# Linear attention on one core: the waits for the last stores, in GpSimd's stream or in SyncE's

## The chip, the cores and the metric

The kernel runs on one core of one Trainium2 chip. The metric is the device time of one execution in microseconds (us); several executions are made and their median is given.

## The reference

For 32 heads of 2048 rows and 128 columns in bf16, the kernel computes linear attention with the feature map elu(x) + 1:

```python
phi_q = jnp.where(q > 0, q + 1, jnp.exp(q)) + 1e-6
phi_k = jnp.where(k > 0, k + 1, jnp.exp(k)) + 1e-6
kv  = jnp.einsum("bhsd,bhse->bhde", phi_k, v)
z   = jnp.einsum("bhsd->bhd", phi_k)
num = jnp.einsum("bhqd,bhde->bhqe", phi_q, kv)
den = jnp.einsum("bhqd,bhd->bhq", phi_q, z)[..., None] + 1e-6
return num / den
```

Each head reads 512 KB each of q, k and v and writes 512 KB of output.

## The kernel before

Each head is one pass of the same operations. Its 2048 rows are laid out as 128 partitions with 16 rows each. SyncE (SP in the profile) issues every DMA of the kernel: 96 loads (`ldq`, `ldk`, `ldv`, line 324) and 34 stores (`st`, line 418). ScalarE (ACT) takes the exponentials of k and of the transposed q, a part of the positive parts, and the copy of the small matrix kv out of PSUM. VectorE (DVE) finishes the feature maps and, at the end of a head, takes the reciprocal of the denominators (line 403) and multiplies (line 410) into the output buffer. GpSimd (POOL) does two things for each head: `v1`, a copy of v beside a column of ones (line 350), and `rkp`, the positive part of half of k (line 346). TensorE (PE) makes kv (line 357), transposes q (line 368) and makes the numerators with their denominators (lines 389 to 396).

The order of every engine's work is written out by hand in `ORDER`, one string for each engine. POOL's string ends with `v131.0 rkp31.0`, the preparation of the last head's k and v. SP's string ends with the stores `st20.0` to `st30.0` and then the three partial stores of the last head, `st31.0 st31.1 st31.2`. `Program.resolve` turns the dependences into waits on semaphores: every engine has one semaphore of its own, and every DMA buffer has one. `Program.emit` writes each engine's stream, with `wait_ge` ahead of the instruction that needs it. There are five independent streams, and a wait holds only what stands behind it in its own stream.

There are twelve output buffers (NO = 12), and so twelve store semaphores, `o0` to `o11`. Head h uses buffer h mod 12; each store adds 16 to its buffer's semaphore when it has landed. After all streams are written, lines 433 to 435 add twelve waits, one for each store semaphore at its final count, the last one for `o7`, the buffer of head 31. They are the last instructions of the kernel; nothing of the kernel stands behind them. The compiler puts two waits into one instruction, so that six EVENT_SEMAPHORE instructions come out of the twelve. In the trace the last two of them wait for `o11` with `o1`, and for `o7` with `o0`.

Of the kernel before, what the change touches and what calls it, by code (L numbers as in the profile page):

```python
# [240 lines left out]
def bass_standalone__linear_attn_elu__prompt_kernel(nc: bass.Bass, q: bass.AP, k: bass.AP, v: bass.AP, out: bass.AP):  # L241
# [11 lines left out]
    with ExitStack() as es:  # L253
# [24 lines left out]
        pr = Program(sem)  # L278
# [153 lines left out]
            pr.emit(e, engine)  # L432
        last = f"o{(NH - 1) % NO}"
        for name in [f"o{s}" for s in range(NO) if f"o{s}" in pr.count and f"o{s}" != last] + [last]:
            nc.sync.wait_ge(pr.get(name), pr.count[name])


# [26 lines left out]
```

## Time and profile before

| what | value |
|---|---|
| median of 5 runs | 170.31 us (169.68 to 170.90) |
| the profiled execution's own time | 169.93 us |
| its span, from the first to the last instruction | 168.5 us |
| busy share of the span | PE 94%, DVE 92%, ACT 91%, POOL 51% |
| granted TensorE clock | 1.00 |
| DMA | 401 GB/s as a mean over the span |

The span is what the profile shows of the kernel's own instructions. The time of the execution is about 1.4 us longer, for what lies around the span. Waits and DMA issues are not counted as busy. The engine names carry a "q" (SPq, POOLq) where an instruction is one of the engine's sequencer alone, such as a wait or a DMA issue.

### The profile page before, as it was taken

The numbers are of one execution on the slowest core, as the hardware profiler recorded it, in microseconds if no ns is written. First come the engines' busy times: TensorE is split into PE (matmuls) and PEld (weight loads), VectorE is DVE, ScalarE is ACT, GpSimd is POOL, SyncE is SP. The second block draws the span as 40 slices with busy tenths as digits, with TensorE's granted clock in tenths as the row PEclk, the third lists the DMA queues.
The fourth block names the chain that finished last, engine by engine and source line by source line (L and its number), as shares of the span: only waits on it lengthen the run. The fifth ranks groups of instructions, "written<-read, shape, count | busy, mean of one in ns | idle before, by whom it ended". The sixth has DMA issues, their size and how long they took to land.

```text
span 168.5 us, 6310 instructions
## 1 busy us (share of the span) xinstructions
PE 159.2 (94%) x2775; PEld 153.4 (91%) x2775; DVE 154.3 (92%) x267; ACT 153.9 (91%) x133; POOL 86.8 (51%) x71
## 2 busy tenths in 40 slices
PE   6989889999999999999999999999999999999960
PEld 2579879999999999999999999999999999999950
DVE  0178999999999999999999999999999999999893
ACT  3799989999999999999999999999999999997810
POOL 1446826556655556556555566555655565445000
PEclk9999999999999999999999999999999999999999
DMA  5999999999999999999999999999999999999986
GB/s 196 381 417 413 409 405 409 409 407 409 415 414 411 408 413 418 415 414 422 406 416 413 414 419 414 411 418 414 421 411 421 412 414 420 414 416 415 396 332 239
DMA packets 18748, 67.53 MB, mean 401 GB/s; under 512 B 2080, under 2 KB 2464, under 8 KB 18720
## 3 DMA queue, kind: packets, MB, share of 16 engines
q1 hardware_dynamic: 18720, 67.12, 98.7%
q8 instruction: 22, 0.36, 0.8%
q14 instruction: 6, 0.05, 0.1%
HBM read 50.33 MB, written 16.78 MB: 398 GB/s over the span
## 4 chain that ended last, share of the span: by engine, by line
PE 83%; DVE 10%; ACT 4%; issue 1%; POOL 0%; POOLq 0%
PE la L357 31%; PE la L394 18%; PE la L396 16%; PE la L368 15%; DVE la L410 5%; ACT la L336 2%; PE la L315 2%; DVE la L342 1%; DVE la L339 1%; ACT la L372 1%; PE la L389 1%; DVE la L374 1%; DVE la L403 1%; DVE la L381 1%; ACT la L378 1%
## 5 line engine op out<-in xcount | busy, mean ns | idle before, releaser
L410 DVE TENSOR_TENSOR la<-la 128x1536 bf16<-128x1536 f32 (+2 forms) x65 | 77.5, 1194 | 0.2
L396 PE MATMUL la<-la 128*128 128x129 bf16 x512 | 68.1, 220 | 0.0
L394 PE MATMUL la<-la 128*128 128x129 bf16 x512 | 68.0, 219 | 0.0
L372 ACT ACTIVATE la<-la 128x2048 bf16<-128x2048 bf16 (+2 forms) x35 | 60.3, 1732 | 5.4 <-PE la L368 3.3
L357 PE MATMUL la<-la 128*128 128x129 bf16 x1024 | 64.0, 219 | 0.7 <-DVE la L339 0.7
L350 POOL COPY la<-la 128x1024 int32<-128x1024 int32 (+1 forms) x33 | 41.7, 1264 | 38.4 <-DVE la L403 29.3
L336 ACT ACTIVATE la<-la 128x2048 bf16<-128x2048 bf16 (+1 forms) x33 | 61.3, 1862 | 0.0
L357 PEld LDWEIGHTS la<-la 128*128 128x128 bf16 x1024 | 60.0, 97 | 1.3 <-DVE la L339 0.8
L346 POOL TENSOR_SCALAR la<-la 128x1024 bf16<-128x1024 bf16 x32 | 44.5, 1392 | 29.0 <-DVE la L410 24.9
L396 PEld LDWEIGHTS la<-la 128*128 128x128 bf16 x512 | 49.5, 97 | 0.0
L394 PEld LDWEIGHTS la<-la 128*128 128x128 bf16 x512 | 47.1, 97 | 0.0
L389 PE MATMUL la<-la 128*128 128x3 bf16 (+1 forms) x192 | 32.3, 168 | 2.4 <-DVE la L410 1.6
L368 PE MATMUL la<-la 128*128 128x128 bf16 x512 | 33.7, 219 | 0.4 <-DVE la L381 0.4
L378 ACT ACTIVATE la<-la 128x1024 bf16<-128x1024 bf16 (+1 forms) x32 | 33.6, 1049 | 0.0
L368 PEld LDWEIGHTS la<-la 128*128 128x128 bf16 x512 | 29.3, 97 | 1.3 <-DVE la L381 0.5
L339 DVE TENSOR_SCALAR la<-la 128x2048 bf16<-128x2048 bf16 (+1 forms) x33 | 23.2, 704 | 3.2 <-ACT la L336 3.2
L389 PEld LDWEIGHTS la<-la 128*128 128x128 bf16 x192 | 18.7, 97 | 3.6 <-DVE la L410 2.3
L374 DVE TENSOR_SCALAR la<-la 128x2048 bf16<-128x2048 bf16 (+2 forms) x35 | 21.2, 608 | 0.3 <-ACT la L372 0.3
L342 DVE TENSOR_SCALAR la<-la 128x1024 bf16<-128x1024 bf16 x32 | 17.1, 534 | 4.5 <-DMA la<-in_k_dram 4.5
L381 DVE TENSOR_SCALAR la<-la 128x1024 bf16<-128x1024 bf16 x31 | 20.8, 670 | 0.0
L403 DVE RECIPROCAL la<-la 128x12 f32<-128x12 f32 (+2 forms) x65 | 12.7, 196 | 2.2 <-PE la L396 0.9
L362 ACT ACTIVATE la<-la 128x129 bf16<-128x129 f32 x32 | 9.0, 282 | 0.4 <-PE la L357 0.4
(14 smaller groups left out, 11.7 us busy)
## 6 DMA issues: line engine op xcount, KB each, us to landing
la<-in_q_dram SPq DMA_DIRECT2D x32, 512.0 KB, 15.5
la<-in_k_dram SPq DMA_DIRECT2D x32, 512.0 KB, 15.3
la<-in_v_dram SPq DMA_DIRECT2D x32, 512.0 KB, 15.3
out_dram<-la SPq DMA_DIRECT2D x31, 512.0 KB, 15.2
out_dram<-la SPq DMA_DIRECT2D x2, 192.0 KB, 2.5
out_dram<-la SPq DMA_DIRECT2D x1, 128.0 KB, 2.6
```

What stands on the lines that cost most here:

```text
L336: add("ACT", f"ek{h}.{i}", lambda e, a=a, b=b: e.activation(em_sb[:, h % NE, a:b], k_sb[:, h % NI, a:b], ACT.Exp), over("ldk", h, ld_parts ...
L339: add("DVE", f"em{h}.{i}", lambda e, a=a, b=b: e.tensor_scalar(em_sb[:, h % NE, a:b], em_sb[:, h % NE, a:b], 1.0, EPS, op0=ALU.min, op1=AL ...
L346: add("POOL", f"rkp{h}.{i}", lambda e, a=a, b=b: e.tensor_scalar(rk_sb[:, h % NR, a:b], k_sb[:, h % NI, a:b], BIG, 0.0, op0=ALU.min, op1=A ...
L350: add("POOL", f"v1{h}.{i}", lambda e, a=a, b=b: e.tensor_copy(v1_sb[:, h % NV, a:b, 0:D].bitcast(i32), v_sb[:, h % NI, a:b].bitcast(i32)), ...
L357: ins = e.matmul(kv_ps, lhsT=src[:, j], rhs=v1_sb[:, h % NV, j, 0:NC], start=(j + part == 0), stop=(j == NT - 1 and part == 1))
L368: ins = e.transpose(xT[:, j], q_sb[:, h % NI, j], ident[:])
L372: add("ACT", f"eq{h}.{i}", lambda e, a=a, b=b: e.activation(emq_sb[:, h % NQ, a:b], xT[:, a:b], ACT.Exp), over("T", h, t_parts, a, b) + fr ...
L378: add("ACT", f"rqa{h}", lambda e: e.activation(rq_sb[:, h % NQ, 0:n], xT[:, 0:n], ACT.Relu), over("T", h, t_parts, 0, n) + freed(NQ, h, (" ...
L389: e.matmul(_ap(o_ps[:, :], o + D, [[NC, m]]), lhsT=ones[:], rhs=epsr[:, 0:m], start=True, stop=False, skip_group_check=True)
L394: e.matmul(to, lhsT=emq_sb[:, h % NQ, t], rhs=kvs_sb[:, h % NK], start=False, stop=False, skip_group_check=True)
L396: ins = e.matmul(to, lhsT=rq_sb[:, h % NQ, t], rhs=kvs_sb[:, h % NK], start=False, stop=True, skip_group_check=True)
L410: return e.tensor_tensor(out=_ap(o_sb[:, :, :, :], first(o_sb[:, h % NO, t0, 0:1]) - first(o_sb[:, :, :, :]), [[m * D, nb], [D, m], [1, D] ...
```

## The change

One word is changed. The same twelve waits, for the same semaphores and the same counts in the same order, are written into GpSimd's stream behind its last operation `rkp31.0`, and no longer into SyncE's behind its last store `st31.2`. SyncE's stream then ends with the issue of that store. Nothing else differs.

```diff
         last = f"o{(NH - 1) % NO}"
         for name in [f"o{s}" for s in range(NO) if f"o{s}" in pr.count and f"o{s}" != last] + [last]:
-            nc.sync.wait_ge(pr.get(name), pr.count[name])
+            nc.gpsimd.wait_ge(pr.get(name), pr.count[name])
```

## The prediction

> **What bounds the kernel now.** I read the page first, then only its last 20 us, because the moved waits are the last instructions of a stream: how many, when they run, what releases them, and what the engine that takes them is doing then. On the page, POOL's row of 40 slices of 4.2 us ends in three zeros, while DMA is busy to the end:
>
> ```profile
> span 168.5 us, 6310 instructions
> ...
> POOL 1446826556655556556555566555655565445000
> ...
> DMA  5999999999999999999999999999999999999986
> ```
>
> The table of windows gives the same with numbers. Each engine's entry is its busy time and, in brackets, its instructions: POOL has none after 156 us, and after 166 us no engine has any; only the stores are under way.
>
> ```profile
> 156.00:164.00 8.00, 6.52 (x120) 6.20 (x117) 7.19 (x13) 3.94 (x5) 0.00 (x0) 1.00 0.90 361
> 164.00:166.00 2.00, 0.16 (x3) 0.00 (x0) 1.83 (x5) 0.00 (x0) 0.00 (x0) 1.00 0.86 329
> 166.00:168.50 2.50, 0.00 (x0) 0.00 (x0) 0.00 (x0) 0.00 (x0) 0.00 (x0) 1.00 0.52 188
> ```
>
> The timeline (start, duration) has POOL's last operation, from 153.51 to 154.93 us, the last two multiplications on DVE, and three of the last stores' issues on SP:
>
> ```profile
> 153.51 1.41 POOL L346 TENSOR_SCALAR la<-la 128x1024 bf16<-128x1024 bf16 x1 [0.45 <-DVE la L410]
> ...
> 164.17 2.02 SPq L418 DMA_DIRECT2D out_dram<-la  x3
> 164.30 1.53 DVE L410 TENSOR_TENSOR la<-la 128x768 bf16<-128x768 f32 x2
> ```
>
> Then the answer for line 435, SP's waits, and the page's row for the last store:
>
> ```profile
> L435 SPq EVENT_SEMAPHORE  x6: 27/28/28, 167.2 to 168.5; - x6
> ```
> ```profile
> SPq L435 <- DMA out_dram<-la: 2.0, 2, 1.0
> ```
> ```profile
> out_dram<-la SPq DMA_DIRECT2D x1, 128.0 KB, 2.6
> ```
>
> Six instructions of 28 ns, the first at 167.2 us and the last at 168.5 us; they stood 2.0 us in all for two landings (1.0 us each) and not at all for the others. So **the end is set by** DVE's last multiplication (ends 165.83), the issue of `st31.2` (165.86 to 166.19), its landing (168.465 by the trace's semaphore records, 2.6 us after the issue began) and the wait that it releases (starts 168.481, ends 168.509). The waits themselves are 6 x 28 = 168 ns, of which only the last 28 ns lie behind the landing.
>
> **What surrounds the span.** The profiled execution took 169.93 us, 1.42 us over its span. The trace's semaphore records run on past the span: the last is at 169.938, equal to that time within 0.01 us. I read from this that the clock stops at the end of the closing barriers, and that what the streams do there counts. The barrier's semaphore has these updates (us from the span's start; the names are my reading of the order):
>
> ```
> first closing barrier:  164.340 PE, 164.374 ACT, 164.412 POOL, 165.987 DVE, 168.624 SP,
>                         then back: 168.667, 168.706, 168.740, 168.787
> second closing barrier: 169.581, .615, .653, .696, .720, then back: .819, .857, .891, .938
> ```
>
> In the first, four updates came early, one by one, as PE, then DVE, ran out of work (DVE's 156 ns after its last multiplication). The fifth came 115 ns after SP's last wait, and four more followed at 34 to 47 ns. In between the user semaphores are reset.
>
> **What the Trainium skill says.** "Runtime: NRT & Kernel Launch", section "The ~15µs preamble/postamble breakdown", describes a closing barrier, a reset of 51 semaphores by each engine and another barrier, and prices the barrier as a serpentine over the five engines at 44 ns a hop. The trace agrees on the form and the hop (34 to 47 ns); the reset took 0.61 us here (168.751 to 169.356) where the page says about 1.5. "Perfetto Trace Analysis", section "Summary: the profiler window per engine type", says that a sequencer's instruction shows only its execution, with the wait hidden ahead of it. That agrees with the 28 ns instructions and their 1.0 us of waiting, and it is why a long wait on POOL won't show as busy time. "DMA: Bandwidth & Descriptors", section "Why a DMA increments its semaphore by 16 and not by 1", says that each DMA engine adds one to the semaphore after its own data has landed; which engine of the core watches the semaphore is no part of the transfer. The trace has POOL and DVE wait on DMA semaphores of transfers that SP issued, so that works.
>
> **The change part by part.**
>
> *Removed from SP:* six instructions x 28 ns. Five lie ahead of the last landing (167.16 to 167.46) and are hidden by it; 28 ns and the 16 ns wake-up lie on the end path. No DMA is issued or moved, and nothing of SP's stands behind them. SP reaches the closing barrier after 166.19 and waits there.
>
> *Added to POOL:* six instructions behind `rkp31.0`, reached at about 154.95 us. The trace has POOL execute one with a single semaphore in 17 ns and one with two in 43 ns (line 217 has 17/17/43). It will pass pairs whose stores have landed and stand at the others; buffers `o0` to `o6` get their last stores between 159.35 and 167.15, and by 168.4 only `o7` is open. Five x 43 = 215 ns are hidden by the 1.0 us between the last two landings. Behind the waits POOL has no work, issues no DMA, and nobody of the kernel waits for it. No transfer, buffer release or other engine moves, so everything up to 168.465 stays.
>
> *The end path:* landing to POOL's wait 24 ns (ten such cases on POOL; SP 16), the wait 43 (SP 28): +23 ns.
>
> *The barrier:* POOL now comes third in a row of five but last in time. Before, its step was long done and SP's arrival at once began the way back. Now POOL's arrival is passed to DVE (+43 ns, as in the second barrier), to SP (+24), and then comes the turn (99 ns in the second barrier, where DVE too has just stepped) in place of the 43 ns of the first. Extra: 43 + 24 + 99 - 43 = **+123 ns**.
>
> *POOL's step out of its stream:* SP needs 115 ns from its last wait to its update. POOL's is not shown: it followed ACT's update by 38 ns after 9.5 us of idleness. Bounds: below, 60 ns, about half of SP's 115, the quickest seen here; above, the whole hidden 9.5 us. The nearest rows are SP's 115, DVE's 156 and POOL's own DRAIN at the opening:
>
> ```profile
> L449 POOLq DRAIN  x1: 187/187/187, 0.3 to 0.3; - x1
> ```
>
> I take 187, so +72 ns (-55 at the low bound).
>
> Sum: 23 + 123 + 72 = **+0.22 us**, against the profiled execution 169.93 + 0.22 = 170.15 us, with the span itself +0.02. This execution lay 0.38 us under the median, so the forecast stands on the median: 170.31 + 0.22 = 170.53, rounded to **170.5 us**, +0.13%. The measurement can tell about 0.5% (0.85 us) from no change; this lies inside.
>
> **The rivals.**
>
> *No part of the closing counts (chance 0.3):* the time ends with the last landing, or POOL's exit is as quick as SP's. Then +0 to +0.1 us, 170.3 to 170.4. For it: the landing is the same in both. Against: the agreement of 169.93 with the last record.
>
> *Slower, POOL's exit is long (chance 0.08):* POOL may have closing work of its own (its cores, or instructions to be fetched: the page has a queue of six instruction packets, one of them at 165.3 us). Before, up to 9.5 us of it was hidden between 154.93 and 164.41. If it begins only after the last wait, it is exposed. It decides when the exit exceeds 115 + 850 - 146 = about 0.82 us. A fetch priced like the kernel's shortest DMA round trip, 2.2 us, gives 170.31 + 0.15 + 2.2 - 0.1 = 172.6. Against: POOL steps through the second barrier in 38 ns, and it stands 12 us in its waits, time enough to fetch ahead.
>
> *Faster (chance 0.03, by spread):* SP's exit leaves the path. At most the 159 ns of its wake-up, last wait and exit could be saved, and POOL's own steps take their place; with a 60 ns exit the sum is still +0.09. Nothing here reaches 0.85 us; only the spread of the runs (169.68 to 170.90) could.
>
> *The edit does nothing:* if the compiler moved the waits to another stream, 170.3. The six instructions under line 435 tell.
>
> **How the numbers follow.** The likeliest, a shift of +0.1 to +0.3 us, has 0.57 and the case of no shift 0.30: 0.87 within 0.5%. The long exit has 0.08; the spread of the runs alone could carry the result over the bound, 0.02 upward and 0.03 downward. The five runs reach 0.63 below and 0.59 above their median, so I take 0.7 on both sides: **169.8 to 171.2 us**; the long exit is left out. Chances: faster 0.03, same 0.87, slower 0.10.
>
> **What would show it.** Right: six EVENT_SEMAPHORE of line 435 on POOLq, the first long before 167 us, the last about 25 ns after the last landing and 43 ns long; none on SPq; span 168.5 plus run-to-run spread; 0.2 us more between span and time (1.42 to about 1.6). Wrong: a gap between span and time of 2.2 us or more (the long exit), an unchanged 1.42 (no shift), or other engines' work before 165.8 us running differently.

## The result, and the profile after

| | before | after |
|---|---|---|
| median | 170.32 us (80 runs) | 170.92 us (43 runs) |
| ratio to before | | 1.0035, 95% interval 1.0024 to 1.0045 |
| the profiled execution's own time | 169.93 us | 170.99 us |
| its span | 168.51 us | 169.15 us |

The change costs 0.35%, which is 0.60 us (0.41 to 0.77). That is inside the 0.5% that the prediction called no change, and inside its range. It is nearly three times the +0.22 us forecast, and the interval of the ratio lies clear of the +0.13% that this would have been.

The span, three windows by engine (busy time, instructions in brackets), and SP's waits for the last 20 us, all of the kernel after:

```profile
span 169.2 us, 6310 instructions
```
```profile
156.00:164.00 8.00, 6.52 (x120) 6.21 (x117) 7.27 (x13) 3.94 (x5) 0.00 (x0) 1.00 0.84 339
164.00:166.00 2.00, 0.42 (x8) 0.24 (x5) 2.00 (x5) 0.00 (x0) 0.00 (x0) 1.00 0.92 358
166.00:169.20 3.20, 0.00 (x0) 0.00 (x0) 0.09 (x1) 0.00 (x0) 0.00 (x0) 0.88 0.46 168
```
```profile
SPq L418 <- DVE la L403: 12.2, 4, 4.7
SPq L418 <- DVE la L410: 3.5, 3, 2.6
```

The last stretch has the same shape: but for the end of DVE's last multiplication every engine has run out, and only stores are under way. That end comes 0.26 us later than in the kernel before (166.089 us against 165.831). It doesn't follow the moved waits: over the five kernels whose last wait stands on POOL it lies between 165.55 and 166.35 us, on both sides of the kernel before. SP still waits for DVE before its stores (line 418), much as before:

```profile
SPq L418 <- DVE la L403: 12.6, 4, 4.3
SPq L418 <- DVE la L410: 3.6, 3, 2.6
```

Line 435 is gone from SP's list after the change. The view of line 435 has it on POOL:

```profile
L435 POOLq EVENT_SEMAPHORE  x6: 42/43/43, 167.8 to 169.1; - x6
```

There are six instructions of 43 ns, where SP had 28. The first starts at 167.8 us and not early: the compiler's first pair is `o6` with `o5`, and `o6` lands at 167.82. The page's row for the last store has 3.0 us from issue to landing, against 2.6 before:

```profile
out_dram<-la SPq DMA_DIRECT2D x1, 128.0 KB, 3.0
```

The span is therefore a trap here. It is 0.64 us longer, almost the measured loss, but only 23 ns of that come from the moved wait; the rest is when the last store landed (169.086 us, against 168.465). Over all the profiles of this study that store took from 1.9 to 3.4 us, and the kernel of the first experiment below, which loses nothing, has its last landing at 169.068.

What repeats is the time that lies outside the span. Timed runs have their spans on record, to 0.1 us. The time less the span is 1.25 to 1.47 us in the 94 runs of the kernel before that were timed beside the experiments (mean 1.31), and 1.79 to 2.00 us in the 44 runs of the kernel after whose spans are on record (mean 1.87). The two don't overlap, and the means differ by 0.56 us, while the spans themselves average 169.0 us in both. So the loss lies outside the span, as far as these means can tell.

The profile shows where the time goes, in the stretch from the last landing to the last record of the closing barriers. These are the trace's semaphore records, counted from the last landing; the engines' names rest on the order of the updates, which the experiments below bear out:

```
                                        before     after
last wait ends                          0.044      0.067 us
POOL's update of the first barrier     -4.053      0.599
SP's update                             0.159      0.666
PE's update, on the way back            0.322      0.883
last record (second barrier)            1.473      2.028
```

The difference at the end is **0.555 us**, against 0.60 us (0.41 to 0.77) from the timed runs. Its parts: 23 ns by the end of the last wait; then 532 ns from there to POOL's update, where SP needed 115 ns, so +417 ns; then 284 ns from that update to PE's return where SP's took 163, so +121 ns; the remainder is 6 ns shorter. So all but 23 ns of the loss lies behind the last instruction that the profile shows.

### The profile page after: what moved, and what is told of

Read it like the earlier page. It is cut to its first block, busy times and chain, and to the rows that moved or that the text cites. A ratio compares the mean times of both kernels' runs of the same rounds, so it can differ in the third digit from the quotient of the medians.

```text
span 169.2 us, 6310 instructions
## 1 busy us (share of the span) xinstructions
PE 159.1 (94%) x2775; PEld 153.4 (91%) x2775; DVE 155.1 (92%) x267; ACT 153.9 (91%) x133; POOL 85.5 (51%) x71
## 4 chain that ended last, share of the span: by engine, by line
PE 54%; ACT 22%; DVE 20%; issue 2%; POOL 0%; POOLq 0%; DVEq 0%
PE la L357 20%; PE la L394 11%; PE la L368 10%; PE la L396 10%; DVE la L410 10%; ACT la L336 9%; ACT la L372 9%; ACT la L378 4%; DVE la L381 3%; DVE la L374 2%; PE la L315 2%; DVE la L339 2%; DVE la L403 2%; DVE la L342 1%; ACT la L362 1%
## 5 line engine op out<-in xcount | busy, mean ns | idle before, releaser
L350 POOL COPY la<-la 128x1024 int32<-128x1024 int32 (+1 forms) x33 | 40.0, 1215 | 43.5 <-DVE la L403 21.5
L339 DVE TENSOR_SCALAR la<-la 128x2048 bf16<-128x2048 bf16 (+1 forms) x33 | 25.1, 761 | 3.3 <-ACT la L336 3.3
L381 DVE TENSOR_SCALAR la<-la 128x1024 bf16<-128x1024 bf16 x31 | 20.8, 670 | 0.0
L342 DVE TENSOR_SCALAR la<-la 128x1024 bf16<-128x1024 bf16 x32 | 16.2, 507 | 4.4 <-DMA la<-in_k_dram 4.4
```

What stands on the lines that cost most here:

```text
L339: add("DVE", f"em{h}.{i}", lambda e, a=a, b=b: e.tensor_scalar(em_sb[:, h % NE, a:b], em_sb[:, h % NE, a:b], 1.0, EPS, op0=ALU.min, op1=AL ...
L350: add("POOL", f"v1{h}.{i}", lambda e, a=a, b=b: e.tensor_copy(v1_sb[:, h % NV, a:b, 0:D].bitcast(i32), v_sb[:, h % NI, a:b].bitcast(i32)), ...
```

## The experiments

My theory: the loss is POOL's long exit from its stream (0.53 us) and its place in the barrier, both behind the last landing. Two rivals: POOL standing in waits disturbs the kernel's own work, or any engine other than SP pays such an exit. The table has what the records of one profile of each kernel gave, in ns. "Exit" runs from the end of the last wait to that engine's update (in e7 and e8 the added instruction lies within it), "barrier" from there to PE's return, "rest" is the reset and the second barrier. A last wait for one semaphore alone (e1, e5, e6) takes 17 ns. The last column is from the timed runs instead: the mean of time less span, in us, with the number of runs.

| kernel | last wait on | wake-up and wait | exit | barrier | rest | landing to last record | time less span, us (runs) |
|---|---|---|---|---|---|---|---|
| before | SP | 44 | 115 | 163 | 1151 | 1473 | 1.31 (94) |
| after | POOL | 67 | 532 | 284 | 1145 | 2028 | 1.87 (44) |
| e1_split | SP | 34 | 116 | 164 | 1149 | 1463 | 1.32 (14) |
| e2_vector | DVE | 78 | 146 | 242 | 1142 | 1608 | 1.42 (22) |
| e3_scalar | ACT | 59 | 109 | 324 | 1144 | 1636 | 1.46 (22) |
| e4_tensor | PE | 80 | 186 | 357 | 1140 | 1763 | 1.63 (22) |
| e5_pool_last_only | POOL | 41 | 537 | 285 | 1229 | 2092 | 1.85 (22) |
| e6_memset_ahead | POOL | 41 | 532 | 286 | 1150 | 2009 | 1.87 (1) |
| e7_memset_behind | POOL | 67 | 683 | 286 | 1146 | 2182 | 1.85 (1) |
| e8_drain_behind | POOL | 67 | 609 | 286 | 1149 | 2111 | 1.88 (1) |

**e1_split: eleven waits on POOL, the last on SP**

```diff
-            nc.sync.wait_ge(pr.get(name), pr.count[name])
+            (nc.sync if name == last else nc.gpsimd).wait_ge(pr.get(name), pr.count[name])
```

> Eleven waits on POOL as after the change, the last one (o7) back on SP. If the time is lost because POOL's exit of about 0.53 us and its place in the barrier come behind the last landing, POOL is now done at about 168.4 us, before SP, and the loss is gone: ratio to before 1.000 (within 0.002), POOL's barrier update some 0.53 us after its own last wait but ahead of SP's, and 1.47 us from the last landing to the last record, as before. If POOL standing in waits disturbed the kernel's work, the loss stays: about 1.003.

Measured: ratio 1.0002 (0.9985 to 1.0019), and the closing, from the last landing to the last record, took 1.463 us. Line 435:

```profile
L435 POOLq EVENT_SEMAPHORE  x6: 17/43/43, 166.5 to 168.2; - x6
L435 SPq EVENT_SEMAPHORE  x1: 17/17/17, 169.1 to 169.1; - x1
```

POOL's last wait ends 0.856 us ahead of the last landing and its update comes 0.324 us ahead of it. The exit is 532 ns again, but now it lies under the last store. Eleven of the twelve store semaphores are still watched by POOL, and nothing is lost, in the ratio or in the time less span (1.32 us against 1.31): the first rival falls. What costs is who is last.

**e2_vector, e3_scalar, e4_tensor: all twelve waits on DVE, ACT or PE**

The three edits differ in the engine alone; the comment here names the other two:

```diff
-            nc.sync.wait_ge(pr.get(name), pr.count[name])
+            nc.vector.wait_ge(pr.get(name), pr.count[name])    # e3: nc.scalar, e4: nc.tensor
```

> All twelve waits on DVE. If the long exit is POOL's own, DVE pays its 156 ns exit (SP 115), a slower wait (+10 to 20 ns) and a shorter detour in the barrier (SP +24, turn 97 in place of 43: +78 ns): +0.13 us behind the last landing, 1.60 us in place of 1.47, ratio 1.001. If any engine other than SP pays 0.5 us to leave its stream after a wait: +0.5 us, 1.003.

> All twelve waits on ACT. If the long exit is POOL's own, ACT pays an exit of 0.11 to 0.16 us and a detour one hop longer than POOL's (38 + 121 = 159 ns): +0.16 to +0.22 us, 1.63 to 1.70 us behind the last landing, ratio 1.001. If any engine other than SP pays 0.5 us: +0.6 us, 1.0035.

> All twelve waits on PE, the first in the barrier. If the long exit is POOL's own, PE pays about 0.18 us of exit (+0.06), a wait some 35 ns slower, and the longest detour (34 + 159 = 193 ns): +0.29 us, 1.76 us behind the last landing, ratio 1.0017. If any engine other than SP pays 0.5 us: +0.65 us, 1.004.

Measured: ratios 1.0004 (0.9989 to 1.0020), 1.0022 (1.0007 to 1.0037) and 1.0020 (1.0005 to 1.0035). The closings were 1.61, 1.64 and 1.76 us; expected were 1.60, 1.63 to 1.70, and 1.76. Line 435 of each, one view from each kernel in that order:

```profile
L435 DVEq EVENT_SEMAPHORE  x6: 49/50/50, 167.8 to 169.1; - x6
```
```profile
L435 ACTq EVENT_SEMAPHORE  x6: 38/38/38, 167.2 to 168.7; - x6
```
```profile
L435 PEldq EVENT_SEMAPHORE  x6: 51/51/51, 167.4 to 168.8; - x6
```

The same wait for two semaphores takes 28 ns on SP, 38 on ACT, 43 on POOL, 50 on DVE and 51 on PE, and none of that is large. The exits of DVE, ACT and PE are 146, 109 and 186 ns: the second rival falls, the long exit is POOL's own. The barrier costs by place. It goes PE, ACT, POOL, DVE, SP and back. The counts show this order: with SP last, four updates of the first barrier come ahead of the last landing, with DVE last three, with POOL two, with ACT one and with PE none. So the last one to arrive has to be followed by all behind it: 163 ns for SP, 242 for DVE, 284 for POOL, 324 for ACT, 357 for PE. The intervals of the ratios alone couldn't separate these three from each other; ACT's and PE's lie clear of 1. The mean of time less span does: 1.42, 1.46 and 1.63 us, in the order of their closings.

**e5_pool_last_only: the last wait alone on POOL**

```diff
-            nc.sync.wait_ge(pr.get(name), pr.count[name])
+            (nc.gpsimd if name == last else nc.sync).wait_ge(pr.get(name), pr.count[name])
```

> Only the last wait (o7) on POOL, the other eleven on SP. If the loss is the price of POOL being the last to leave, it is all here with one wait: wake-up 24 ns, a single wait 17 ns, exit 532 ns, barrier as after the change, 2.00 us from the last landing to the last record (2.03 after the change, 1.47 before), ratio 1.003. If the number of waits on POOL mattered, a twelfth to a sixth of the loss: about 1.0005.

Measured: ratio 1.0017 (1.0002 to 1.0033), closing 2.09 us.

```profile
L435 SPq EVENT_SEMAPHORE  x6: 17/28/28, 166.8 to 168.4; - x6
L435 POOLq EVENT_SEMAPHORE  x1: 17/17/17, 169.4 to 169.4; - x1
```

One wait on POOL buys the whole exit, 537 ns. The closing is 0.09 us over what was expected mostly because the reset and second barrier took 1.229 us in this one execution, against 1.14 to 1.15 elsewhere. The timed ratio is below the expected 1.003, which is still within its interval. Its spans happened to be 0.20 us shorter on average than those of the kernel before (168.87 against 169.07 us). The time less span is 1.80 to 1.93 us in every one of its 22 runs, 0.54 us above the kernel before in the mean, so the loss is here with one wait.

**e6_memset_ahead, e7_memset_behind, e8_drain_behind: what the exit waits for**

Three edits of the kernel after, shown in one listing. Each kernel has only the lines that its comment names; e6 and e7 also have the spare tile:

```diff
+        spare = sb([P, 1])
 ...
+            if name == last:
+                nc.gpsimd.memset(spare[:], 0.0)      # e6, ahead of the last wait
             nc.gpsimd.wait_ge(pr.get(name), pr.count[name])
+        nc.gpsimd.memset(spare[:], 0.0)              # e7 instead; e8: nc.gpsimd.drain()
```

> All twelve waits on POOL, and a memset of one column of a spare tile on POOL just ahead of the last wait, about 0.9 us before the last landing. If POOL's exit is long because its cores have been idle for 14 us, it falls well below 0.53 us, toward the 0.11 to 0.19 us of the other engines. If it is a fixed series of steps of POOL's sequencer, it stays at 0.53 us and the closing at 2.03 us.

> All twelve waits on POOL, and a memset of one column of a spare tile behind the last wait. If the exit contains a wait for POOL's cores to be empty, POOL's barrier update comes after the memset's end (about 0.06 us to start and 0.1 us to run) plus most of 0.53 us: 0.70 to 0.76 us behind the landing (0.60 after the change). If the exit is the sequencer's alone and doesn't look at the cores, the memset runs beside it: 0.60 to 0.65 us.

> All twelve waits on POOL, and an explicit DRAIN of POOL behind the last wait. If most of the exit is a drain of POOL, the page shows what one takes with idle cores (187 ns at the opening, behind four memsets), and what follows gets shorter by it: POOL's update stays near 0.60 us behind the landing. If the drain is a small thing beside the exit's other steps, it adds its own length, 0.1 to 0.2 us: 0.70 to 0.80 us.

Each was executed once, for its profile (169.97, 171.15 and 170.08 us: single times can't be compared). The added instructions, in the order e6, e7, e8:

```profile
L437 POOL MEMSET la<- x1: 101/101/101, 167.3 to 167.3; 128x1 bf16 x1
```
```profile
L437 POOL MEMSET la<- x1: 102/102/102, 169.2 to 169.2; 128x1 bf16 x1
```
```profile
L436 POOLq DRAIN  x1: 41/41/41, 168.2 to 168.2; - x1
```

POOL's cores do its operations, such as a memset (POOL in the views); its sequencer does its waits and drains (POOLq). In e6 the cores had worked 0.73 us before the last landing, and the exit stayed at 532 ns, as expected of a fixed series of steps: 14 us of idleness aren't its cause. In e7 POOL's update came 0.750 us behind the landing, inside the 0.70 to 0.76 expected of an exit that waits for the cores. That is 151 ns later than after the change and 512 ns behind the memset's end, so the exit did not run beside the memset. Its time less span is no longer than after the change because the span now ends with the memset. In e8 POOL's update came 0.676 us behind the landing, 77 ns later than after the change. Neither expected figure was met (0.60, or 0.70 to 0.80), because the drain took 41 ns where 100 to 200 were supposed. 524 ns of exit still followed it, so that an explicit drain takes no more than 8 ns off the exit. With one profile each, e7 and e8 show this once.

The prediction named one more candidate, a fetch of instructions. In the five kernels with POOL last, the trace's last packet of an instruction queue ends at 165.3 to 166.1 us, at least 2.7 us before POOL's last wait ends, and no DMA packet of any kind is on record after the last landing. The kernel before has such a packet too, ending at 165.6 us. So no record speaks for a fetch by DMA. What POOL does in the half microsecond isn't shown by any record here and stays open.

## Why the prediction was right or wrong, point by point

- **The kernel's own work doesn't move:** right within what the runs can tell. The split kernel (e1) has the ratio 1.0002, and the mean spans of before and after differ by less than 0.1 us.
- **The last wait costs 23 ns more on POOL:** measured 23 ns (67 against 44).
- **The early waits are hidden:** right. But the sign given for it, the first of them long before 167 us, did not come: they are passed at most 1.3 us before the last landing, all after `o6` lands. The prediction had POOL passing pairs one by one as stores land; the compiler's pairing puts `o6` first. The trace of the kernel before had this already: SP's first wait there starts at 167.164 us, 17 ns after `o6` landed.
- **The barrier's detour, 123 ns:** measured 121 ns. The records of the second barrier of the kernel before were enough to price it. The quoted agreement with the Trainium skill's hop is looser than it reads: "Runtime: NRT & Kernel Launch", section "The ~15µs preamble/postamble breakdown", gives the 44 ns for the opening barrier, and the hops of the closing barriers run from 23 to 47 ns over all profiles, with turns of 43 to 44 or 97 to 100.
- **POOL's exit, 187 ns by its opening DRAIN:** this is the step of the prediction that failed. The mechanism was right and the term was mis-sized: it is 532 ns, 345 ns more, and 0.22 + 0.345 is 0.565 us, the measured 0.555 us but for 10 ns. The DRAIN was the wrong row: behind the last wait of e8 a DRAIN took 41 ns, and hardly anything came off the exit for it. The bounds were honest (60 ns to 9.5 us), but the value was taken from the low end, and the case of a long exit was given a price of 2.2 us with little between. The forecast's likeliest shift of +0.1 to +0.3 us failed; the true exit lies between it and the rival. That the measured 170.92 us still falls inside the range is luck as far as the exit goes: the range was drawn from the spread of five runs and left a long exit out.
- **No part of the closing counts (0.3):** refuted, by the ratio's interval and by the 0.56 us in time less span. The time of the profiled execution is the last record less 0.12 to 0.13 us in the kernel after and all eight experiments (171.114 against 170.99 after), while the closing went from 1.46 to 2.18 us: the clock takes the closing in. The agreement within 0.01 us in the kernel before, on which the prediction read this, was closer than in all the others. The conclusion was right, but one profile was thin ground for it.
- **The gap between span and time:** forecast 1.6 us, measured 170.99 - 169.15 = 1.84 us, and 1.87 in the mean of the runs. The 1.42 us of the profile before, from which the forecast started, was itself high for that kernel (mean 1.31), so the two profiles alone show a growth of 0.42 us where the runs show 0.56.
- **The range and the chances:** same (within 0.5%) holds at 1.0035, but the mark of 0.5% is near the interval's end of 1.0045.

## What to carry to other kernels

The last wait of a kernel isn't free to stand anywhere: what its engine does between that wait and the closing barrier, and its place in the barrier, come behind the last landing. Here SP is the cheapest last engine and POOL the dearest; earlier waits may stand on POOL if it is done early enough before the last one (0.86 us in e1; its exit of 532 ns and one hop of 43, less the 150 ns that SP took from the landing to its update in e1, make about 0.4 us, an estimate that no run tried). And when an engine has been idle long before the end, the trace of before bounds its exit badly: price it widely, or read it from a kernel where that engine is last. When a change can only act outside the span, compare time less span run by run: here that parted before and after without overlap, where the times themselves, spread over 1.7 us before, needed dozens of runs.

## What the runs showed of the hardware that was not expected

- POOL needs 532 to 537 ns from its last wait to its update in the closing barrier (after, e1, e5, e6); SP 115, ACT 109, DVE 146, PE 186.
- Its update follows the end of POOL's last instruction by about that time, whether this is a wait (532 ns), a memset (512, e7) or a drain (524, e8), and work of the cores 0.73 us before the last landing (e6) doesn't shorten it.
- The last 128 KB store took 1.9 to 3.4 us from issue to landing over ten profiles of kernels with the same stores, so the span of one profile can't show a change of half a microsecond.
